# Two of the four sums of weights of a pair of column tiles are written into the plain weights' PSUM buffers

## The chip, the core and the metric

One core of a Trainium2 chip runs the kernel. The metric is the device time of one execution in microseconds (us); the kernel's time is the median of three executions. The engines are PE (matmuls; PEld are its weight loads), DVE, ACT and POOL, which work on tiles of 128 partitions, and SP, which issues the DMAs. SBUF is the working memory. PSUM is the memory that PE writes its sums to; in this kernel DVE and ACT also read and write it, POOL does not.

## What is computed

Causal attention (2 x 12 heads, 448 rows, 64 columns each), a gated layer with RMS norm (768 to 1536 and back) and a layer with a squared ReLU (768 to 2048 and back), all in float32:

```python
scores = scale * np.matmul(q, k.transpose(0, 1, 3, 2))
...
attn = attn / (np.sum(attn, axis=-1, keepdims=True) + 1e-09)
return np.matmul(attn, v).astype(np.float32)
...
xn = x / rms * rms_g
g = xn @ w_gate
silu = g * (1.0 / (1.0 + np.exp(-g)))
val = xn @ w_val
return (silu * val @ w_out).astype(np.float32)
...
h = np.maximum(x @ w_in, 0.0)
return (h * h @ w_out).astype(np.float32)
```

## The kernel before

**Numbers in two parts.** A float32 operand is split into a rounded high part and the rest (the low part), and each product of a weight tile with an activation tile is three matmuls of 128x128 by 128x448: high-high, high-low, low-high. `form` (called 7 times per pair of weight tiles, below) makes the parts of a weight: a cast for the high part (line 241 on ACT, 239 on POOL) and a subtraction for the low part (line 637, on DVE or POOL), both into one of 8 buffers `ring`. `parts` does the same for an activation tile (high: lines 241 and 239; low: line 526, on DVE or POOL), into `part`.

**Seven products for eight.** `halves` takes two column tiles of a weight matrix (a and b, each 768 rows by 128 columns of it, laid out as 128 partitions x 768, and split into halves a11, a12 and a21, a22) and multiplies them with the activations in a scheme with seven block products instead of eight. It needs four sums of weights:

```python
s1 = minus(a21, a22, da + 3, plus=True)
s2 = minus(s1, a11, da + 4)
...
s3 = minus(a11, a21, da + 6)
...
s4 = minus(a12, s2, da + 9)
```

The seven products of a pair stand on PE in the order p1 (a11), p2 (a12), p6 (s2), p5 (s1), p7 (s3), p4 (a22), p3 (s4), nine matmuls each. There are 29 such pairs: 10 for the gate and value matrices, 5 for the first output matrix, 8 for the second layer's input matrix `w2i`, 6 for its output matrix; one pair (the first) uses other buffers. The other column tiles are multiplied plainly (`whole_tiles`, `whole`).

**Where the weights lie.** The weights come as raw 8-byte pairs by DMA into `raw` (2 buffers). `weights` turns them back into float32: two ACT activations (line 600 into the plain buffer, line 605 inside `raw`) and a DVE step (line 610). The plain buffer is one of two called `s`: 1024 columns in PSUM each, of which 768 are used; a takes one, b the other. The half a21 alone goes into an `st` buffer instead (5 buffers in SBUF, 384 columns each), so that a sum of two weights always has one operand in PSUM and one in SBUF: its half of b's PSUM buffer holds an intermediate that is dead once a21 is made. The four sums (`minus`, line 664, always on DVE when an operand is in `s`) go into `st` as well. So a pair takes five `st` buffers. A `form` whose source is in `st` may run its high part on ACT or POOL and its low part on DVE or POOL. From a source in `s` the high part runs on ACT and the low part on DVE alone.

**What else is on DVE and POOL.** Differences of activations (`differences`, line 681), additions of a finished PSUM sum (banks `m`) to what came before (lines 723, 767, 938, 991), the gate's steps (lines 773 to 795), the squared ReLU (line 1001). Lines 723 and 938 also free a bank, and PE waits for them when it goes on in that bank.

**What sets the order.** `Order` is a planner that runs when the program is built: each step has a due time, the engines it may run on with an assumed cost each, what it waits for and which buffers it takes; the planner goes through assumed time and writes each engine's instructions in a fixed order. It also keeps a term for the port of SBUF that DVE and POOL share (`port=True`, set for a step whose operands are all in SBUF). An engine then runs its instructions strictly in that order, so an edit to one step can move everything behind it. All transfers are issued from SP's queue.

Of the kernel before, what the change touches and what calls it, by code (L numbers as in the profile page):

```python
# [17 lines left out]
B, H, S, D = 2, 12, 448, 64  # L18
DM, DF1, DF2 = 768, 1536, 2048
P = 128  # L20
# [25 lines left out]
class Order:  # L46
# [8 lines left out]
    def buf(self, pool):  # L55
        return Buf(pool)
# [5 lines left out]
    def add(self, due, opts, f, after=(), new=(), uses=(), mode=None, begin=0.0, prev=(), port=False):  # L62

        t = dict(due=due, opts=opts, f=f, port=port, after=[a for a in after if a], new=list(new), uses=list(uses) + list(new),
                 mode=mode, begin=begin, end=None, eng=None, i=len(self.tasks), prev=[a for a in prev if a])
        for b in t["uses"]:
            b.left += 1
        self.tasks.append(t)  # L70
        return t

    def chain(self, due, opts, f, after=(), new=(), prev=(), **kw):

        t = self.add(due, opts, f, after, new, prev=[self.last.get(b.pool) for b in new] + list(prev), **kw)
        for b in new:
            self.last[b.pool] = t
        return t
# [90 lines left out]
def tile_attention_moe_moe2(ctx: ExitStack, tc: tile.TileContext, qk, v, wg, wv, wo, w2i, w2o, rms_g, out):  # L169
# [29 lines left out]
    add, chain, buf = order.add, order.chain, order.buf  # L199
# [34 lines left out]
    def E(c):  # L234
        return {"A": nc.scalar, "D": nc.vector, "P": nc.gpsimd}[c]
# [18 lines left out]
    for i, fill in enumerate((1.0, -1.0e9 * float(D) ** 0.5)):  # L254
        for k in range(2):
            for sl in (slice(0, D), slice(D, P)):
                t = half[sl, 2 * i + k]
# [8 lines left out]
    for i in range(NV):  # L266
        t = atc.tile([P, 4, 2 * D], F32, name=f"vt{i}")
# [3 lines left out]
    for i in range(2):  # L271
        t = atc.tile([P, 2, 512], F32, name=f"p2t{i}")
# [14 lines left out]
    def D_(n):  # L287
        return 0.15 + n / 960

    def P_(n, two=False):  # L290
        return 0.2 + 0.0021 * n if two else 0.22 + 0.0009 * n
# [363 lines left out]
        return add(due, {"E": 0.61 * n}, f, [tw] + [x[1] for x in xs[:n]] + list(after), new=[bank] if first else [],  # L655
                   uses=[bw] + [x[0] for x in xs[:n]] + ([] if first else [bank]), mode="f")

    def minus(a, b, due, plus=False):

        bs = buf("st")  # L660

        def f(e):
            x, y = (t[0].tile[:, t[1]:t[1] + 3 * P] for t in (a, b))
            (E(e).tensor_add if plus else E(e).tensor_sub)(bs.tile, x, y)  # L664

        sb = "s" not in (a[0].pool, b[0].pool)
        t = chain(due, {**({"P": P_(3 * P, True)} if sb else {}), "D": D_(3 * P)}, f, [a[2], b[2]], new=[bs],
                  uses=[a[0], b[0]], port=sb)
        return bs, 0, t

    def differences(x, due, prev=(), both=False):

# [25 lines left out]
    def halves(a, b, f, due, done, scale=1.0, begin=0.0, home="s", sums=None, end=False):  # L698
# [4 lines left out]
        da = due - 18  # L703
        ca, t = weights(a, NCC, da, begin, home)
        a11, a12 = (ca, 0, t), (ca, 3 * P, t)
        a21, a22 = weights(b, NCC, da + 1, begin, home, True)
        fa11, fa12 = form(a11, 3, da + 2), form(a12, 3, da + 2)
        s1 = minus(a21, a22, da + 3, plus=True)
        s2 = minus(s1, a11, da + 4)
        fs2, fs1 = form(s2, 3, da + 5), form(s1, 3, da + 5)  # L710
        s3 = minus(a11, a21, da + 6)
        fs3 = form(s3, 3, da + 7)
        fa22 = form(a22, 3, da + 8)
        s4 = minus(a12, s2, da + 9)
        fs4 = form(s4, 3, da + 10)
        x, z, y = buf("m"), buf("m"), buf("m")

# [25 lines left out]
        if end:  # L743
            sums[0][1] = k4 = snap(x, p7, due + 9 - SOON, 1, 0)
            x = buf("m")
# [123 lines left out]
    for k in range(2 * NE):  # L869
        due = 40 + 8.0 * k  # L870
        c, t = weights((wg, wv)[k % 2][k // 2], NCC, due, due, "wt")
# [8 lines left out]
    f = differences(xf, 1012.0)  # L880
    f.update(B11=xs[0][:3], B21=xs[0][3:], B22=xs[1][3:])
    due = 1020.0
# [96 lines left out]
    due = seven(wo, 0, g, yf, due)  # L979
    hx = halved(hf, NCC, highs(g))  # L980
    due = seven(wo, NCC, hx, yf, due, n=NCC // 2 - 1)
    hy = [[parts(hf[1][NCC + i], due - 5 + i, highs(hx)) for i in range(3)]]
    due = whole(wo, NCC, NCC, [hx["B11"] + hx["B21"], hy[0] + hx["B22"]], yf, due, NCC - 2)
    f = halved(yf, 0, highs(hy))
# [32 lines left out]
    due = whole(w2o, 0, 4, hx, of, due)  # L1017
    f = halved(h2, 4, highs(hx), True)
    due = seven(w2o, 4, f, of, due)
    g = halved(h2, 10, highs(f))  # L1020
    due = seven(w2o, 10, g, of, due, True)
# [43 lines left out]
```

## Time and profile before

| | |
|---|---|
| median of 3 executions | 562.68 us (559.97, 562.68, 563.57) |
| the profiled execution | 564.28 us, of which the span from first to last instruction is 562.5 us |
| PE / PEld busy | 545.7 us (97%) / 475.4 us (85%) |
| DVE busy | 495.5 us (88%) |
| ACT / POOL busy | 379.6 us (67%) / 280.8 us (50%) |
| granted TensorE clock, whole span | 0.997 of full speed (2.4 GHz) |

A matmul is pipelined: it is shown as 367 ns long on average, while the next starts about 0.2 us after it. PE's busy share therefore hides short stops. The number of matmuls that start in a stretch of time is the better measure of PE's pace. The attention takes the first 117 us; the matmuls of line 652 (all the big products) follow until 558.6 us.

### The profile page before, as it was taken

The numbers are of one execution on the slowest core, as the hardware profiler recorded it, in microseconds if no ns is written. First come the engines' busy times: TensorE is split into PE (matmuls) and PEld (weight loads), VectorE is DVE, ScalarE is ACT, GpSimd is POOL, SyncE is SP. The second block draws the span as 40 slices with busy tenths as digits, with TensorE's granted clock in tenths as the row PEclk, the third lists the DMA queues.
The fourth block names the chain that finished last, engine by engine and source line by source line (L and its number), as shares of the span: only waits on it lengthen the run. The fifth ranks groups of instructions, "written<-read, shape, count | busy, mean of one in ns | idle before, by whom it ended". The sixth has DMA issues, their size and how long they took to land.

```text
span 562.5 us, 8893 instructions
## 1 busy us (share of the span) xinstructions
PE 545.7 (97%) x3056; PEld 475.4 (85%) x3056; DVE 495.5 (88%) x862; ACT 379.6 (67%) x802; POOL 280.8 (50%) x322
## 2 busy tenths in 40 slices
PE   7999999999899999999999999899999999999997
PEld 4666666899899999999989789789999999999896
DVE  4778988699998998999999999999888887999983
ACT  4678888566766666668787576666766876758510
POOL 4466776343630442147488488331212871687710
PEclk9899999999999999999999999999999999999999
DMA  6255323303233333344253143025432344431422
GB/s 180 83 174 188 113 67 128 114 2 113 89 136 114 113 112 118 123 141 132 106 162 119 57 158 123 2 112 174 148 128 76 112 144 128 160 103 66 145 84 82
DMA packets 19501, 65.06 MB, mean 116 GB/s; under 512 B 2048, under 2 KB 8960, under 8 KB 19456
## 3 DMA queue, kind: packets, MB, share of 16 engines
q1 hardware_dynamic: 19376, 64.27, 34.4%
q8 instruction: 24, 0.39, 0.3%
q10 hardware_dynamic: 80, 0.23, 0.2%
q14 instruction: 21, 0.17, 0.1%
HBM read 61.74 MB, written 2.75 MB: 115 GB/s over the span
## 4 chain that ended last, share of the span: by engine, by line
PE 68%; DVE 23%; issue 3%; POOL 3%; ACT 2%; DMA 1%; POOLq 0%; ACTq 0%; DVEq 0%
PE m L652 53%; DVE ring L637 6%; DVE part L526 5%; PE t L439 3%; PE o L477 3%; PE s L336 3%; PE s L852 2%; PE s L349 2%; DVE st L664 2%; DVE row L681 2%; DVE row L938 2%; DVE s L610 2%; POOL p L423 1%; ACT ring L241 1%; DVE row L723 1%
## 5 line engine op out<-in xcount | busy, mean ns | idle before, releaser
L652 PE MATMUL m<-part,ring 128*128 128x448 f32 x2115 | 436.0, 367 | 5.6 <-DVE part L526 2.4
L652 PEld LDWEIGHTS m<-part,ring 128*128 128x128 f32 x2115 | 395.9, 188 | 45.6 <-DVE part L526 4.6
L526 POOL TENSOR_TENSOR part<-row,part 128x448 fp32r<-128x448 f32 x78 | 99.3, 1292 | 45.9 <-ACT part L241 44.9
L681 POOL TENSOR_TENSOR row<-row 128x448 f32<-128x448 f32 x52 | 65.6, 1276 | 25.4 <-DVE row L792 19.7
L241 ACT CAST ring<-st 128x384 fp32r<-128x384 f32 x93 | 46.4, 512 | 35.7 <-DVE st L664 25.4
L605 ACT ACTIVATE raw<-raw 128x768 uint32<-128x768 uint8 (+1 forms) x70 | 62.6, 894 | 11.1 <-DMA raw<-in_wv 4.4
L637 DVE TENSOR_TENSOR ring<-st,ring 128x384 fp32r<-128x384 f32 x96 | 68.1, 736 | 1.5 <-ACT ring L241 1.1
L241 ACT CAST part<-row 128x448 fp32r<-128x448 f32 x111 | 58.9, 570 | 14.0 <-DVE row L681 11.4
L239 POOL TENSOR_SCALAR ring<-st 128x384 fp32r<-128x384 f32 x23 | 12.4, 537 | 108.7 <-DVE st L664 62.7
L600 ACT ACTIVATE s<-raw 128x768 f32<-128x768 f32 (+1 forms) x64 | 54.1, 849 | 10.2 <-DVE ring L637 8.8
L241 ACT CAST ring<-s 128x384 fp32r<-128x384 f32 x100 | 43.9, 469 | 18.3 <-DVE s L610 9.6
L526 DVE TENSOR_TENSOR part<-row,part 128x448 fp32r<-128x448 f32 x62 | 54.7, 902 | 0.7 <-POOL part L239 0.4
L610 DVE SCALAR_TENSOR_TENSOR s<-s,raw 128x768 uint32<-128x768 uint32 (+1 forms) x64 | 48.6, 760 | 3.7 <-ACT s L600 2.4
L637 DVE TENSOR_TENSOR ring<-s,ring 128x384 fp32r<-128x384 f32 x100 | 51.2, 531 | 0.5 <-ACT ring L241 0.3
L282 ACT COPY snap<-m 128x448 f32<-128x448 f32 x47 | 25.0, 532 | 29.7 <-PE m L652 29.0
L372 DVE TENSOR_REDUCE mx<-s 128x2 f32<-128x256 f32 (+2 forms) x36 | 23.8, 687 | 14.0 <-PE s L352 9.0
L423 POOL TENSOR_SCALAR p<-p,r 128x128 f32<-128x128 f32 (+1 forms) x48 | 24.3, 524 | 20.8 <-DVE r L413 18.0
L664 DVE TENSOR_TENSOR st<-st,s 128x384 f32<-128x384 f32 x56 | 30.7, 548 | 1.1
L664 DVE TENSOR_TENSOR st<-s,st 128x384 f32<-128x384 f32 x56 | 30.0, 548 | 0.3 <-ACT ring L241 0.2
L637 POOL TENSOR_TENSOR ring<-st,ring 128x384 fp32r<-128x384 f32 x20 | 21.7, 1087 | 15.4 <-ACT ring L241 14.5
L336 PE MATMUL s<-qk 64*128 64x128 f32 (+2 forms) x144 | 27.0, 456 | 1.6 <-DMA qk<-in_qk 0.9
L938 DVE TENSOR_TENSOR row<-m,row 128x448 f32<-128x448 f32 x36 | 22.3, 621 | 5.2 <-PE m L652 4.7
(98 smaller groups left out, 586.6 us busy)
## 6 DMA issues: line engine op xcount, KB each, us to landing
raw<-in_w2i SPq DMA_DIRECT2D x16, 768.0 KB, 4.2
raw<-in_wg SPq DMA_DIRECT2D x12, 768.0 KB, 4.3
raw<-in_wv SPq DMA_DIRECT2D x12, 768.0 KB, 4.3
raw<-in_wo SPq DMA_DIRECT2D x12, 768.0 KB, 4.3
raw<-in_w2o SPq DMA_DIRECT2D x12, 768.0 KB, 4.4
qk<-in_qk SPq DMA_DIRECT2D x11, 448.0 KB, 3.4
raw<-in_w2o SPq DMA_DIRECT2D x6, 512.0 KB, 3.7
out_t<-row SPq DMA_DIRECT2D x12, 224.0 KB, 1.9
```

Of the source, the lines that this page charges most:

```text
L241: eng.copy(o, i)
L336: nc.tensor.matmul(s[:, h, o:o + n], z["qk"][BOTH[h], 0, qs], z["qk"][BOTH[h], 1, :n], start=True, stop=False)
L423: E(e).tensor_scalar(t, t, z["r"][:, k:k + 1], 1.0, ALU.mult, ALU.mult)
L526: E(e).tensor_sub(bs.tile[:, 1], bf.tile, bs.tile[:, 0].bitcast(F32))
L600: nc.scalar.activation(bt.tile[:, :n * P], br.tile[:, :n * P, 1].bitcast(F32), AF.Prelu, scale=2.0 ** -112, alpha=2.0 ** 32)
L605: nc.scalar.activation(br.tile[:, :n * P, 0], b, AF.Copy, scale=1.0 / 32, bias=-31.0 / 64)
L610: nc.vector.scalar_tensor_tensor(dst.tile.bitcast(U32) if dst else u, u, 3, br.tile[:, a:b, 0], ALU.logical_shift_left, ALU.bitwise_or)
L637: E(e).tensor_sub(br.tile[:, 1, :n], num(), br.tile[:, 0, :n].bitcast(F32))
L652: nc.tensor.matmul(bank.tile[:, :S], bw.tile[:, a, i], x[:, c], start=first and i == 0 and k == 0, stop=last and i == n - 1 and k == 2, sk ...
L664: (E(e).tensor_add if plus else E(e).tensor_sub)(bs.tile, x, y)
L681: E(e).tensor_sub(bs.tile, a[0].tile, b[0].tile)
L938: nc.vector.tensor_add(bf.tile, bank.tile[:, :S], snap.tile if snap else bf.tile)
```

## The change

`minus` gets an argument `to`: a place that exists already. With it the sum is written there and takes no `st` buffer. s3 = a11 - a21 goes into the dead half of b's PSUM buffer, after a21 is made; s4 = a12 - s2 goes over a12 in a's PSUM buffer, after a12's low part is made. s1 and s2 stay in `st`. The steps that form s3 and s4 now read PSUM, so each has ACT for its high part and DVE for its low part, and a's buffer is in use until the parts of s4 are made.

```diff
-    def minus(a, b, due, plus=False):
+    def minus(a, b, due, plus=False, to=None):
 
-        bs = buf("st")
+        bs, o = (to[0], to[1]) if to else (buf("st"), 0)
 
         def f(e):
             x, y = (t[0].tile[:, t[1]:t[1] + 3 * P] for t in (a, b))
-            (E(e).tensor_add if plus else E(e).tensor_sub)(bs.tile, x, y)
+            (E(e).tensor_add if plus else E(e).tensor_sub)(bs.tile[:, o:o + 3 * P], x, y)
 
         sb = "s" not in (a[0].pool, b[0].pool)
-        t = chain(due, {**({"P": P_(3 * P, True)} if sb else {}), "D": D_(3 * P)}, f, [a[2], b[2]], new=[bs],
-                  uses=[a[0], b[0]], port=sb)
-        return bs, 0, t
+        opts = {**({"P": P_(3 * P, True)} if sb else {}), "D": D_(3 * P)}
+        if to:
+            t = add(due, opts, f, [a[2], b[2], to[2]], uses=[a[0], b[0]] + ([bs] if bs not in (a[0], b[0]) else []), port=sb)
+        else:
+            t = chain(due, opts, f, [a[2], b[2]], new=[bs], uses=[a[0], b[0]], port=sb)
+        return bs, o, t
...
-        s3 = minus(a11, a21, da + 6)
+        s3 = minus(a11, a21, da + 6, to=(a22[0], 0, a21[2]))
         fs3 = form(s3, 3, da + 7)
         fa22 = form(a22, 3, da + 8)
-        s4 = minus(a12, s2, da + 9)
+        s4 = minus(a12, s2, da + 9, to=(ca, 3 * P, fa12[2]))
```

Lines from 674 on carry higher numbers in the changed kernel: 681 is 684 there, 723 is 727, 938 is 942, 991 is 995, 1001 is 1005. PE's products keep their order. On DVE and POOL the planner moves a good deal.

**First place: DVE around 316 to 325 us**, where the first output matrix changes over from pairs to plain column tiles. Lines 723 and 938 (727 and 942) add a finished sum and free its bank; line 526 is the low part of an activation; line 610 a weight. Before:

```order
L610 SCALAR_TENSOR_TENSOR s<-s,raw 128x768
L526 TENSOR_TENSOR part<-row,part 128x448
L723 TENSOR_TENSOR row<-m,row 128x448
L637 TENSOR_TENSOR ring<-s,ring 128x384
L526 TENSOR_TENSOR part<-row,part 128x448 x3
L723 TENSOR_TENSOR row<-m,row 128x448
L938 TENSOR_TENSOR row<-m,row 128x448
L637 TENSOR_TENSOR ring<-s,ring 128x384
L938 TENSOR_TENSOR row<-m,row 128x448
```

The same stretch in the changed kernel:

```order
L610 SCALAR_TENSOR_TENSOR s<-s,raw 128x768
L727 TENSOR_TENSOR row<-m,row 128x448
L942 TENSOR_TENSOR row<-m,row 128x448
L637 TENSOR_TENSOR ring<-s,ring 128x384
L727 TENSOR_TENSOR row<-m,row 128x448
L637 TENSOR_TENSOR ring<-s,ring 128x384
L526 TENSOR_TENSOR part<-row,part 128x448
L637 TENSOR_TENSOR ring<-s,ring 128x384
L610 SCALAR_TENSOR_TENSOR s<-s,raw 128x768
L942 TENSOR_TENSOR row<-m,row 128x448
```

Before, four low parts of activations stand among these rows, three of them in a row ahead of an addition; now one stands there, and the others have moved to POOL or to other places on DVE.

**Second place: DVE between two pairs of `w2i`** (about 390 to 400 us). Lines 991 and 1001 (995 and 1005) finish a column of the pair that PE is at; line 610 makes the next pair's weights, and the last row its first two low parts. Before:

```order
L610 SCALAR_TENSOR_TENSOR s<-s,raw 128x768
L991 TENSOR_TENSOR row<-m,snap 128x448
L1001 SCALAR_TENSOR_TENSOR row<-row 128x448
L991 TENSOR_TENSOR row<-m,snap 128x448
L1001 SCALAR_TENSOR_TENSOR row<-row 128x448
L610 SCALAR_TENSOR_TENSOR st<-s,raw 128x384
L610 SCALAR_TENSOR_TENSOR s<-s,raw 128x384
L637 TENSOR_TENSOR ring<-s,ring 128x384 x2
```

In the changed kernel:

```order
L995 TENSOR_TENSOR row<-m,snap 128x448
L1005 SCALAR_TENSOR_TENSOR row<-row 128x448
L637 TENSOR_TENSOR ring<-s,ring 128x384
L995 TENSOR_TENSOR row<-m,snap 128x448
L1005 SCALAR_TENSOR_TENSOR row<-row 128x448
L610 SCALAR_TENSOR_TENSOR s<-s,raw 128x768
L610 SCALAR_TENSOR_TENSOR st<-s,raw 128x384
L610 SCALAR_TENSOR_TENSOR s<-s,raw 128x384
L637 TENSOR_TENSOR ring<-s,ring 128x384 x2
```

The step that makes a's weights has moved behind both finished columns, and the low part of s4 of the running pair stands ahead of it, since a's buffer is held until then.

## Rows read from the trace of the kernel before

**Rows 1.** The page, busy time of the engines over the span (us, share, instructions).

```profile
PE 545.7 (97%) x3056; PEld 475.4 (85%) x3056; DVE 495.5 (88%) x862; ACT 379.6 (67%) x802; POOL 280.8 (50%) x322
```

**Rows 2.** Busy time by stretch: us, each engine's time (instructions), clock, DMA.

```profile
150.00:280.00 130.00, 130.00 (x643) 120.45 (x643) 122.18 (x211) 92.38 (x169) 52.27 (x53) 1.00 0.38 128
283.00:367.00 84.00, 80.03 (x379) 69.95 (x379) 82.51 (x123) 59.07 (x110) 57.41 (x50) 1.00 0.30 102
370.00:530.00 160.00, 160.00 (x776) 145.30 (x775) 142.25 (x245) 114.47 (x211) 80.81 (x80) 1.00 0.37 127
```

**Rows 3.** Timeline of PE, unbroken runs: start, length, matmuls [idle before, releaser].

```profile
147.73 163.08 PE L652 MATMUL m<-part,ring 128*128 128x448 f32 x799 [1.42 <-ACT snap L282]
311.21 4.39 PE L652 MATMUL m<-part,ring 128*128 128x448 f32 x20 [0.40 <-DVE part L526]
315.96 2.07 PE L652 MATMUL m<-part,ring 128*128 128x448 f32 x9 [0.36 <-DVE row L938]
318.55 5.79 PE L652 MATMUL m<-part,ring 128*128 128x448 f32 x27 [0.53 <-DVE row L723]
324.57 27.38 PE L652 MATMUL m<-part,ring 128*128 128x448 f32 x133 [0.22 <-DVE row L938]
353.12 4.53 PE L652 MATMUL m<-part,ring 128*128 128x448 f32 x21 [1.17 <-DVE part L526]
...
366.41 166.20 PE L652 MATMUL m<-part,ring 128*128 128x448 f32 x803 [0.41 <-DVE part L526]
532.85 25.78 PE L652 MATMUL m<-part,ring 128*128 128x448 f32 x126 [0.24 <-DVE row L723]
```

**Rows 4.** Timeline of DVE, 309 to 325 us: start, length of the group.

```profile
311.08 0.54 DVE L637 TENSOR_TENSOR ring<-st,ring 128x384 fp32r<-128x384 f32 x1
...
316.59 1.28 DVE L526 TENSOR_TENSOR part<-row,part 128x448 fp32r<-128x448 f32 x1
317.80 0.61 DVE L723 TENSOR_TENSOR row<-m,row 128x448 f32<-128x448 f32 x1
...
318.80 3.53 DVE L526 TENSOR_TENSOR part<-row,part 128x448 fp32r<-128x448 f32 x3
```

**Rows 5.** DVE by shape, whole span: count, busy us, mean ns, idle before.

```profile
L637 DVE TENSOR_TENSOR ring<-st,ring 128x384 fp32r<-128x384 f32 x96 | 68.1, 736 | 1.5 <-ACT ring L241 1.1 <-POOL ring L239 0.4
L526 DVE TENSOR_TENSOR part<-row,part 128x448 fp32r<-128x448 f32 x62 | 54.7, 902 | 0.7 <-POOL part L239 0.4 <-ACT part L241 0.2
L637 DVE TENSOR_TENSOR ring<-s,ring 128x384 fp32r<-128x384 f32 x94 | 49.9, 547 | 0.5 <-ACT ring L241 0.3
...
L610 DVE SCALAR_TENSOR_TENSOR s<-s,raw 128x384 uint32<-128x384 uint32 x28 | 15.7, 562 | 0.6
L1001 DVE SCALAR_TENSOR_TENSOR row<-row 128x448 f32<-128x448 f32 x22 | 15.5, 703 | 0.8
...
L610 DVE SCALAR_TENSOR_TENSOR st<-s,raw 128x384 uint32<-128x384 uint32 x28 | 15.3, 547 | 1.7 <-ACT raw L605 1.7
```

**Rows 6.** DVE by shape, 283 to 367 us only.

```profile
L637 DVE TENSOR_TENSOR ring<-st,ring 128x384 fp32r<-128x384 f32 x18 | 18.0, 1018 | 0.4 <-POOL ring L239 0.4
L526 DVE TENSOR_TENSOR part<-row,part 128x448 fp32r<-128x448 f32 x16 | 16.4, 1046 | 0.0
L637 DVE TENSOR_TENSOR ring<-s,ring 128x384 fp32r<-128x384 f32 x17 | 9.0, 546 | 0.1
...
L610 DVE SCALAR_TENSOR_TENSOR s<-s,raw 128x768 uint32<-128x768 uint32 x7 | 6.7, 958 | 0.0
L681 DVE TENSOR_TENSOR row<-row 128x448 f32<-128x448 f32 x7 | 5.9, 848 | 0.0
L664 DVE TENSOR_TENSOR st<-s,st 128x384 f32<-128x384 f32 x10 | 5.3, 546 | 0.0
```

**Rows 7.** POOL by shape, whole span, the low parts of activations.

```profile
L526 POOL TENSOR_TENSOR part<-row,part 128x448 fp32r<-128x448 f32 x78 | 99.3, 1292 | 45.9 <-ACT part L241 44.9
```

**Rows 8.** Waits by engine and line: us in total, times, longest.

```profile
ACT s L600 <- DVE ring L637: 8.8, 9, 3.4
```

## The prediction

> **What bounds the kernel now.** I began with the busy shares [rows 1]. PE is at 97%, so a change on DVE can give back only what PE stops for, plus whatever changes PE's pace. The question is where PE stops, and for whom.
>
> The table by stretch [rows 2] answers the first half, if matmuls are counted. At a granted clock of 1.00 (the 2.4 GHz level) 643 matmuls fit into the 130 us from 150 to 280, one per 0.2022 us. From 370 to 530 there are 776 in 160 us, one per 0.2062 us (each count is one or two too high at its edges). Between them, 283 to 367, there are 379 in 84 us: at 0.2022 us they need 76.6 us, so 7.4 us are lost. The timeline of PE's unbroken runs [rows 3] shows them as a series of stops from 311 to 366 us, each released by DVE (line 526, 723 or 938), one per row and two rows left out. Outside it there are two stops, at 147.73 (1.42 us idle) and at 532.85 (0.24 us).
>
> The second half: in that stretch DVE is busy 82.51 of 84 us [rows 2], against 122.18 of 130 before it. DVE's queue is the bound there. Why it is so slow there is seen by comparing shapes. Forming a low part from `s` (PSUM) takes 547 ns over the whole span and 546 in the stretch. The same size from `st` (SBUF) takes 736 over the span and 1018 in the stretch [rows 5, 6]. Low parts of activations, also all in SBUF, go from 902 to 1046. So an instruction with both inputs in SBUF loses up to half a microsecond there, and one that reads PSUM loses nothing. One form from `st` that met no POOL work took 0.54 us [rows 4]. POOL does its own SBUF work at that time, 57.41 us of 84 [rows 2]; that the two disturb each other is my reading of these rows.
>
> A third thing matters for the size of any answer: PE has two paces, 0.2022 and 0.2062 us, at the same clock. The slow one holds from the stop at 366.41 to the one at 532.85: 803 matmuls in 166.44 us [rows 3]. 4 ns on 803 matmuls are 3.2 us. I see the pace change only at stops, and nothing in the rows tells which one PE will take.
>
> **The change, part by part.**
>
> *The sums themselves.* 56 sums (28 pairs, s3 and s4; the first pair's buffers lie in SBUF) write PSUM now. Nothing is added or removed. The trace has no subtraction of two weights that writes `s`; its bounds are line 610 into `s`, 562 ns, and into `st`, 547 [rows 5], same size and inputs. So 0 to 15 ns each, 0.8 us over the span at most. I take 0: the ten sums of the bound stretch would cost 0.15 us, and elsewhere DVE's slack of 8 us in 130 [rows 2] hides it. Without that cover it is 0.8 us.
>
> *The forms of s3 and s4.* Their low parts now read PSUM and are DVE's alone. By the instruction orders, DVE's low parts from `st` fall from 96 to 48 and those from `s` rise from 94 to 150. The planner gives POOL other work for what it loses: the low parts of activations on DVE fall from 62 to 47, and POOL's rise from 78 to 93. At 1292 ns [rows 7] the fifteen are 19.4 us more for POOL, which is busy 50% of the span [rows 1].
>
> *What that is worth.* Only the bound stretch counts. Between the addition at 283.3 us and the line 991 at 370.3 us the orders give, for DVE:
> - low parts from `st` 18 to 10: 8 x 1.00 us (18.0 us for 18, [rows 6]) = -8.0
> - low parts from `s` 19 to 30: 11 x 0.53 (9.0 for 17) = +5.8
> - low parts of activations 16 to 11: 5 x 1.03 (16.4 for 16) = -5.1
> - differences, line 681, 7 to 9: 2 x 0.84 (5.9 for 7) = +1.7
> - sums, line 664, 18 to 20: 2 x 0.53 (5.3 for 10) = +1.1
> - one more square (0.70, line 1001, [rows 5]) and two fewer copies (0.61 each, as line 723 of the same size, [rows 4]) = -0.5
>
> That is -5.0 us on a queue that is full. The bounds: if POOL's extra work makes the remaining SBUF instructions dearer in the same measure, nothing is left; if every collision goes with the eight low parts, PE gets back all of its stops. These are below the 7.4 us, since the slow pace has a share of it: 4 ns on 379 matmuls at most, 1.5 us. So the range is 0 to about 6.8.
>
> *Where it arrives.* At 315.96, 318.55 and 324.57 PE waits for additions (lines 938, 723, 938), which free banks [rows 3]. Just ahead of such additions DVE does a low part of 1.28 us at 316.59, and three in 3.53 us at 318.80 [rows 4]. In the new order one stands there instead of four (first place). Those three stops, idle 0.36 + 0.53 + 0.22, are longer by about 0.2 us each, since PE's idle time begins only when the last matmul has drained: about 1.7 us, and I expect nearly all of it back. The one at 311.21 waits for a low part (about 0.6); the new order puts that row ahead of the two low parts from `st` that preceded it, so this one too should go. The later stops: the 133 matmuls from 324.57 to 353.12 need 26.9 of 28.55 us, and the next 54 (21 in their row, 33 in the two rows left out) 10.9 of 13.29 us, so about 4.0 us are lost. There s1 and s2 are still formed from `st`, so I expect half, 2.0 us. Together 1.7 + 0.6 + 2.0 = **4.3 us**, which agrees with the -5.0 from the other side, and I take it.
>
> *What is moved the wrong way.* a's `s` buffer is now held until s4 is formed. ACT already waits for DVE's low parts before it can fill that buffer, 8.8 us in 9 waits [rows 8]. In the new order (second place) the next pair's weights are made after both finished columns. From the end of p5, which releases the second of these additions, PE has p7, p4 and p3 left: 27 matmuls, 5.5 us. DVE needs in that time 0.61 (line 991, as line 723), 0.70 (line 1001), 0.96 + 0.56 + 0.55 (line 610) and 0.53 (the first low part) [rows 4 to 6]: 3.9 us. 1.6 us remain, so this costs nothing as long as nothing else comes between. Before, a's weights were made ahead of the first column, and there was far more room.
>
> *The first stop*, 147.73, stays: the orders there differ by one more low part from `s` ahead of the difference it hangs on (+0.5) and a POOL low part fewer. I take 0. SP's queue moves one load of the last pair behind the first store; the product that needs it comes more than 100 matmuls (20 us) after. Nothing.
>
> *A rule against it.* The Trainium skill, "Perfetto Trace Analysis", section "Optimizing Scalar/DVE Operations", gives DVE an overhead of about 60 ns for SBUF and 125 for PSUM. By it the 10 sums and 11 low parts that go to PSUM in the stretch would cost 65 ns more each, 1.4 us, and 5.0 would be 3.6, an estimate. The rows here show no such step: 546 ns from PSUM [rows 6], and 0.54 us for an undisturbed form from SBUF at 311.08 [rows 4]. The trace disagrees, and I leave the sum.
>
> **The sum.** The profiled execution took 564.28 us (span 562.5). 564.28 - 4.3 = 560.0. It lies 1.6 us above the median of the three, which a difference in pace can explain. Off the median, 562.68 - 4.3 = 558.4, and that is the basis I use: **558.5 us**.
>
> **The rivals.**
> - *No gain.* POOL's 15 more low parts collide with what DVE still does in SBUF, or the pace falls at an early stop: 643 matmuls from 150 to 280 at 4 ns more are 2.6 us. For it: s1 and s2 stay in `st`, and POOL's waits leave it room to come at any time. Against it: eight of 18 exposed forms are gone. Time: 562.0.
> - *Gain and fast pace.* If PE leaves the stops of 353 to 366 at the fast pace, 3.2 us more come off: about 555. For it: the stretch up to 280 ran so. Against: nothing decides it here.
> - *Slower.* The next pair's weights come too late at the second place. It decides when DVE or ACT puts more than the spare 1.6 us into that path, as one collided low part (1.0) and a line 610 (0.96) would. Every pair of the gate, `w2i` and the second half of w2o repeats it: 0.4 us on some 21 pairs are 8 us, 570. Against it: the rows in that path read PSUM and do not lengthen.
> - *PSUM dearer.* If each of the 21 instructions that go to PSUM in the stretch cost a tenth more than the 546 ns of rows 6, the gain is 1.1 us smaller: 559.6. Against it: 562 ns against 547 [rows 5]. The Trainium skill's rule above points this way.
>
> **How the numbers follow.** Forecast 0.55 (its own range 555.5 to 561.5), no gain 0.22, fast pace 0.12, slower 0.08, PSUM dearer 0.03. About 1% (5.6 us) is what a measurement of this kernel can tell from no change: below 557.05 is faster, above 568.3 slower. Faster: the fast pace and three tenths of the forecast, 0.28. Slower: 0.08. The same: 0.64. For 8 in 10 the range takes in the no-gain case with its scatter and the fast pace, and leaves the slower one out: 554.0 to 564.5.
>
> **What would show it.** Right: between 283 and 370 us the low parts from `st` number about 10, PE's stops at 311 to 325 are gone, and the count of matmuls in 84 us rises from 379 towards 400. Wrong: line 526 or 681 on DVE above 1.1 us each there; a repeated stop at every p1 of a pair with ACT's line 600 or DVE's line 610 as releaser; or an equal number of stops with a pace of 0.206 where it was 0.202.

## The result

The changed kernel takes **555.83 us** (median of 7 executions, 553.28 to 559.01) against 562.27 for the kernel before on the same chip (7 executions, 559.97 to 563.71): ratio **0.9899, 95% interval 0.9864 to 0.9934**. It is faster by about 1%, 2.7 us below the forecast and inside the range. Two more measurements of it, in experiments below, gave 0.9939 and 0.9961; why they differ is part of the story. By the three measurements the kernel is faster by 0.4 to 1.0%. Three executions with a mean granted clock of 0.56 to 0.75 and one of the kernel before that took 568.33 us are in no ratio.

The profiled execution of the changed kernel took 555.83 us, of which the span is 553.9. The table by stretch, in the form of [rows 2]:

```profile
150.00:280.00 130.00, 130.00 (x643) 120.36 (x642) 121.24 (x214) 90.59 (x168) 51.37 (x52) 1.00 0.38 126
283.00:367.00 84.00, 82.66 (x408) 76.16 (x407) 81.17 (x130) 61.80 (x116) 64.80 (x58) 1.00 0.34 115
370.00:530.00 160.00, 159.79 (x789) 147.76 (x788) 143.69 (x247) 110.22 (x208) 79.83 (x78) 1.00 0.37 123
```

In the bound stretch 408 matmuls start where 379 did. From 370 to 530 there are 789 for 776, and PE hardly stopped there in either kernel: that is pace. The timeline of PE's unbroken runs, in the form of [rows 3]:

```profile
117.37 29.34 PE L652 MATMUL m<-part,ring 128*128 128x448 f32 x144
148.62 149.87 PE L652 MATMUL m<-part,ring 128*128 128x448 f32 x738 [1.90 <-DVE uu L793]
299.83 177.24 PE L652 MATMUL m<-part,ring 128*128 128x448 f32 x873 [1.34 <-ACT snap L282]
477.27 73.23 PE L652 MATMUL m<-part,ring 128*128 128x448 f32 x360 [0.21 <-DVE row L727]
```

All the stops from 311 to 366 us are gone. Three are left: the first (1.90 for 1.42), a new one at 299.83, and a small one at 477. DVE in the bound stretch, by shape, as in [rows 6]:

```profile
L637 DVE TENSOR_TENSOR ring<-s,ring 128x384 fp32r<-128x384 f32 x30 | 16.3, 548 | 1.6 <-ACT ring L241 1.5
L637 DVE TENSOR_TENSOR ring<-st,ring 128x384 fp32r<-128x384 f32 x10 | 11.1, 1135 | 0.0
L684 DVE TENSOR_TENSOR row<-row 128x448 f32<-128x448 f32 x9 | 8.5, 943 | 0.0
L526 DVE TENSOR_TENSOR part<-row,part 128x448 fp32r<-128x448 f32 x11 | 8.4, 765 | 0.0
...
L664 DVE TENSOR_TENSOR s<-s,st 128x384 f32<-128x384 f32 x10 | 5.6, 557 | 0.0
L664 DVE TENSOR_TENSOR st<-st,s 128x384 f32<-128x384 f32 x10 | 5.5, 549 | 0.1
```

The counts are those of the order (30, 10, 9, 11). A low part made from PSUM takes 548 ns as before. What reads two SBUF operands takes 765 to 1135, and these means moved: the low parts from `st` went from 1018 to 1135, the differences from 848 to 943, the low parts of activations from 1046 to 765. A sum costs 557 ns into `s` and 549 into `st`. ACT's waits for DVE's low parts, which answer to [rows 8]:

```profile
ACT ring L241 <- DVE ring L637: 11.8, 8, 3.0
ACT s L600 <- DVE ring L637: 6.1, 11, 1.0
```

Line 600 waits less than before. Line 241, a cast, waits 11.8 us; in the kernel before it was

```profile
ACT ring L241 <- DVE ring L637: 4.0, 4, 1.9
```

**How the runs are compared.** For each profile I took the starts of the 2115 matmuls of line 652 and split the time from the first to the last into a base (2114 spacings of 202.7 ns and the length of the last matmul, the same 428.9 us in all kernels), what starts more than 230 ns apart lose ("stops", the lower clock included), and what the rest lose against 202.7 ns ("pace"). The two paces can be told by their rhythm: 206, 207, 207 ns evenly, or a cycle of five near 199, 207, 202, 203, 202. In us:

| kernel | ratio to before [95%] | first to last | stops | pace |
|---|---|---|---|---|
| before | | 441.7 | 9.0 | 3.8 |
| before_again | | 441.5 | 9.0 | 3.6 |
| after | 0.9899 [0.9864, 0.9934] | 433.1 | 4.3 | -0.1 |
| after_again | 0.9939 [0.9916, 0.9962] | 436.0 | 7.2 | -0.1 |
| after_third | 0.9961 [0.9932, 0.9989] | 438.3 | 8.4 | 1.0 |
| no_pool | 1.0025 [0.9993, 1.0056] | 443.4 | 10.3 | 4.2 |
| s3_sbuf | 0.9982 [0.9948, 1.0016] | 439.5 | 4.8 | 5.8 |
| s4_only | 0.9979 [0.9953, 1.0006] | 441.2 | 8.5 | 3.7 |
| banks_before | 0.9997 [0.9968, 1.0026] | 444.4 | 8.1 | 7.4 |
| banks_again | 0.9935 [0.9910, 0.9959] | 436.0 | 7.2 | 0.0 |
| late_after | 0.9872 [0.9837, 0.9908] | 435.8 | 4.4 | 2.5 |
| late_banks | 0.9894 [0.9856, 0.9931] | 437.5 | 3.4 | 5.3 |
| late_s3a | 0.9844 [0.9805, 0.9882] | 433.1 | 3.0 | 1.2 |

The ratio is over several executions, the other columns are of the one profiled. Of the 8.6 us between the first and the third row, 4.7 are stops and 3.9 pace. By place, the 4.7 are 6.4 us less at the stops of 311 to 366 us and 0.4 less at small ones near 282, against 0.5 more at the first stop and 1.6 at the new one.

### The profile page after: what moved, and what is told of

Read it like the earlier page. It is cut to its first block, busy times and chain, and to the rows that moved or that the text cites. A ratio compares the mean times of both kernels' runs of the same rounds, so it can differ in the third digit from the quotient of the medians.

```text
span 553.9 us, 8846 instructions
## 1 busy us (share of the span) xinstructions
PE 539.3 (97%) x3056; PEld 476.6 (86%) x3056; DVE 485.9 (88%) x858; ACT 375.1 (68%) x799; POOL 286.0 (52%) x326
## 4 chain that ended last, share of the span: by engine, by line
PE 77%; DVE 15%; ACT 2%; DMA 2%; POOL 2%; issue 2%; POOLq 0%; DVEq 0%; ACTq 0%; SPq 0%
PE m L652 65%; DVE ring L637 4%; PE t L439 3%; PE o L477 3%; PE s L336 3%; DVE part L526 3%; PE s L349 2%; POOL p L423 1%; DVE row L684 1%; DMA raw<-in_wv 1%; DVE row L577 1%; DMA qk<-in_qk 1%; DVE s L610 1%; DVE st L664 1%; DVE mx L370 1%
## 5 line engine op out<-in xcount | busy, mean ns | idle before, releaser
L652 PE MATMUL m<-part,ring 128*128 128x448 f32 x2115 | 429.7, 365 | 3.5 <-DVE uu L793 1.9
L526 POOL TENSOR_TENSOR part<-row,part 128x448 fp32r<-128x448 f32 x93 | 114.6, 1252 | 34.6 <-ACT part L241 31.7
L241 ACT CAST ring<-s 128x384 fp32r<-128x384 f32 (+1 forms) x156 | 69.5, 473 | 35.6 <-DVE s L610 11.9
L637 DVE TENSOR_TENSOR ring<-s,ring 128x384 fp32r<-128x384 f32 (+1 forms) x156 | 80.4, 539 | 6.2 <-ACT ring L241 5.5
L239 POOL TENSOR_SCALAR ring<-st 128x384 fp32r<-128x384 f32 x17 | 8.7, 513 | 114.2 <-DVE st L664 92.6
L526 DVE TENSOR_TENSOR part<-row,part 128x448 fp32r<-128x448 f32 x47 | 37.5, 818 | 0.6 <-POOL part L239 0.4
L637 DVE TENSOR_TENSOR ring<-st,ring 128x384 fp32r<-128x384 f32 x48 | 37.8, 818 | 0.0
L239 POOL TENSOR_SCALAR part<-row 128x448 fp32r<-128x448 f32 x37 | 25.8, 700 | 20.9 <-PE m L652 17.1
L241 ACT CAST ring<-st 128x384 fp32r<-128x384 f32 x41 | 20.1, 511 | 20.6 <-DVE st L664 16.3
L664 DVE TENSOR_TENSOR s<-s,st 128x384 f32<-128x384 f32 x56 | 31.4, 560 | 0.5
```

The lines of the kernel that those rows point to most:

```text
L239: eng.tensor_scalar(o, i, 1.0, 1.0, ALU.mult, ALU.mult)
L241: eng.copy(o, i)
L526: E(e).tensor_sub(bs.tile[:, 1], bf.tile, bs.tile[:, 0].bitcast(F32))
L637: E(e).tensor_sub(br.tile[:, 1, :n], num(), br.tile[:, 0, :n].bitcast(F32))
L652: nc.tensor.matmul(bank.tile[:, :S], bw.tile[:, a, i], x[:, c], start=first and i == 0 and k == 0, stop=last and i == n - 1 and k == 2, sk ...
L664: (E(e).tensor_add if plus else E(e).tensor_sub)(bs.tile[:, o:o + 3 * P], x, y)
```

## The experiments

### Each kernel again

*before_again* is the kernel before, unchanged, run once more.

> The kernel before, once more, for a second profile of it. If PE's pace (one matmul per 0.2022 or 0.2062 us) belongs to the kernel, the stretch 370 to 530 us holds 776 matmuls again and 150 to 280 us holds 643. If it belongs to the single execution, one of the two counts differs: 789 in the first or 631 in the second. The stops between 311 and 366 us should be there in either case, about 6 us in all.

It took 561.96 us. The timeline of PE's unbroken runs shows the same stops, and the same long slow run at the end:

```profile
309.01 4.33 PE L652 MATMUL m<-part,ring 128*128 128x448 f32 x20 [0.86 <-DVE part L526]
...
322.37 27.88 PE L652 MATMUL m<-part,ring 128*128 128x448 f32 x133 [0.22 <-DVE row L938]
350.85 4.53 PE L652 MATMUL m<-part,ring 128*128 128x448 f32 x21 [0.60 <-DVE part L526]
...
364.14 166.17 PE L652 MATMUL m<-part,ring 128*128 128x448 f32 x803 [0.50 <-DVE part L526]
```

803 matmuls in 166.17 us answer to 803 in 166.20 [rows 3], and the stretches of [rows 2] hold 643 and 776 matmuls again. So in these two executions the pace of the long runs repeated. It is not fixed throughout: the 133 matmuls after 322.37 took 27.88 us here and 27.38 before.

*after_again* and *after_third* are the changed kernel, unchanged, on the chips of the other experiments.

> The changed kernel, once more. If its gain is in the stops alone, 556 us again (ratio 0.99) with three stops, at about 148, 300 and 477 us, whatever the pace. If the fast pace of its first profile was luck, this profile shows 776 instead of 789 matmuls from 370 to 530 us or 631 instead of 643 from 150 to 280 us, and its span is 2 to 6 us longer.

> The changed kernel once more, beside the two layouts. Two of its executions ran wholly at the fast pace of 202.7 ns a matmul. If the pace belongs to the kernel's order, it does so again, with stops at matmuls 144, 882 and 1755 alone, and the time is 0.990 to 0.994 of before. If the pace is drawn anew at each stop, some hundred matmuls may run at 206.7 ns here: up to 4 us longer, 0.997.

They are 0.9939 and 0.9961. The pace is the fast one again (a loss of -0.1 and 1.0 us), the stops at 300 and 477 us are there again; what differs is the first stop. In after_third, PE's run behind the stop:

```profile
148.23 153.74 PE L652 MATMUL m<-part,ring 128*128 128x448 f32 x738 [3.18 <-DVE uu L793]
```

The timeline of DVE ahead of it:

```profile
141.80 2.93 DVE L637 TENSOR_TENSOR ring<-st,ring 128x384 fp32r<-128x384 f32 x2
```

And PE's table by stretch behind the stop:

```profile
148.00:153.00 5.00, 4.77 (x13) 4.27 (x14) 4.21 (x8) 3.18 (x6) 2.00 (x2) 0.50 0.12 28
153.00:158.00 5.00, 5.00 (x24) 4.51 (x23) 2.36 (x5) 1.83 (x4) 1.34 (x2) 0.88 0.80 288
```

The same table for the first profile of the changed kernel, where the stop was 1.90 us:

```profile
148.00:153.00 5.00, 4.38 (x22) 4.10 (x23) 4.59 (x8) 3.97 (x8) 1.61 (x2) 1.00 0.17 22
153.00:158.00 5.00, 5.00 (x26) 4.64 (x25) 4.37 (x9) 2.77 (x6) 1.77 (x2) 1.00 0.75 292
```

After a stop of 3.18 us the granted clock is 0.50 (the 1.2 GHz level) from 148 to 153 and 13 matmuls start, not 22. After the 1.90 us it stayed at 1.00. Counted by the starts of the matmuls, 2.1 us are lost there in the first profile and 5.0 and 6.1 in after_again and after_third (1.7 in the kernel before).

It is DVE that is late. It reaches line 793 30.5 us after the first matmul of line 652 in the first profile and 31.8 us in after_third. The same two low parts from `st` took, in the first profile,

```profile
142.54 1.97 DVE L637 TENSOR_TENSOR ring<-st,ring 128x384 fp32r<-128x384 f32 x2
```

That is 1.0 us less than in after_third, but the low part of an activation behind them took 0.6 us more (1.57 for 0.97). The other 1.0 us lies 13 us earlier: one low part of an activation takes 1.58 us on DVE in after_third and 0.62 in the first profile. In both, a low part on POOL starts 0.15 us ahead of it; POOL's took 1.25 us in after_third and 2.26 in the first profile. So the same two instructions met, and it was now the one, now the other engine that lost the time.

The executions without a profile show only their mean granted clock. Of the 29 executions of this kernel (the three profiled ones among them) 12 have 0.993 or 0.994, with a mean span of 558.2 us; the other 17 have 0.996 or more and 555.2. That mean is a rough sign, since it also holds a fall of the clock in the attention that some executions have: the first profile's 0.996 comes from 13 to 18 us, where the clock is 0.66. In after_again the two low executions are no longer than the other eight (555.9 against 556.3). So the profiles show what the longer stop costs, 2.8 and 4.0 us; how much of the spread of the three ratios it makes is not shown.

### Is it POOL alone?

*no_pool*: the sums stay in SBUF, but the forms of s3 and s4 may not go to POOL, as in the change.

```diff
-    def form(src, n, due):
+    def form(src, n, due, pool=True):
...
-        sb = b.pool != "s"
+        sb = b.pool != "s" and pool
...
-        fs3 = form(s3, 3, da + 7)
+        fs3 = form(s3, 3, da + 7, False)
...
-        fs4 = form(s4, 3, da + 10)
+        fs4 = form(s4, 3, da + 10, False)
```

> The kernel before, all four sums in SBUF, but the planner may not put the forms of s3 and s4 on POOL. Planner theory (POOL is freed for the low parts of activations): most of the gain, 557 to 558. Port theory: nothing or a loss, since DVE gets more work with both inputs in SBUF: 562 to 566.

1.0025: no gain, the time that the port theory expected. Its table by stretch:

```profile
150.00:280.00 130.00, 127.67 (x617) 115.24 (x616) 122.24 (x206) 87.48 (x157) 53.32 (x54) 1.00 0.36 122
283.00:367.00 84.00, 82.99 (x401) 74.22 (x400) 81.94 (x130) 57.27 (x107) 64.14 (x58) 1.00 0.35 117
```

The bound stretch is nearly as good as in the changed kernel (401 for 408), but 26 matmuls are missing from 150 to 280, and there are 10.3 us of stops in all. The planner's new order only moved the stops.

### The order of after, with s3 in SBUF

*s3_sbuf* keeps the instruction order of the changed kernel. s3 is written to an SBUF tile of its own (`sh`) and formed from there; s4 stays in PSUM. (Two tiles of four columns in the norm also share one buffer now.) The part of the edit that writes s3:

```diff
+            if to and bs.pool == "s" and o == 0:
+                sh[bs, o] = pw.tile([P, 3 * P], F32, tag=f"sh{o}", name="sh", bufs=1)
+                E(e).tensor_sub(sh[bs, o], x, y)
+                return
...
```

> The changed kernel with its instruction order, only that s3 is written to an SBUF tile of its own and formed from there; s4 stays in PSUM. Port theory (the forms that read PSUM no longer collide with POOL): about 5 of the 15 low parts moved in the bound stretch are exposed again at 1.0 instead of 0.55 us, so 2 to 3 us on DVE come back there: about 558.5. Planner theory (what counts is the order that the planner made): no change, 556. It also takes away the wait of a22's high part for s3's low part, which by itself would give up to 1.6 us (554).

DVE by shape in 283 to 367 us (line 641 is 637 of the changed kernel):

```profile
L641 DVE TENSOR_TENSOR ring<-s,ring 128x384 fp32r<-128x384 f32 x24 | 13.0, 547 | 0.8 <-ACT ring L241 0.8
...
L526 DVE TENSOR_TENSOR part<-row,part 128x448 fp32r<-128x448 f32 x11 | 9.5, 859 | 0.0
...
L641 DVE TENSOR_TENSOR ring<-sh,ring 128x384 fp32r<-128x384 f32 x6 | 5.7, 953 | 0.0
```

One run of PE:

```profile
314.53 173.69 PE L656 MATMUL m<-part,ring 128*128 128x448 f32 x837 [1.51 <-DVE row L735]
```

This is the price of the place, at the same order: a low part of s3 takes 953 ns from SBUF where others take 547 from PSUM, 2.4 us on six, and the eleven of line 526 take 859 where they took 765, 1.1 more. It comes back as one stop of 1.51 us at 314.53, for a DVE addition. But the stop at 300 us is not there, so all stops together are 4.8 us, hardly more than in the changed kernel. Of the 6.5 us that the kernel before lost from 311 to 366 us, 2.0 are lost here: the order keeps the rest away, also with s3 in SBUF. Whether it would with both sums in SBUF was not run. The time, 560.42 us (0.9982), is above all that were expected; in the profiled execution the reason is 5.8 us of slow pace.

### One of the two sums

*s4_only*: s4 goes into PSUM, s3 stays in SBUF, and the planner makes its own order. Against the kernel before, with `minus` as in the change:

```diff
-        s4 = minus(a12, s2, da + 9)
+        s4 = minus(a12, s2, da + 9, to=(ca, 3 * P, fa12[2]))
```

> Half of the change: s4 alone goes to PSUM, s3 stays in SBUF, and the planner makes its own order (DVE low parts from st 96 to 76, from s 100 to 128, activation low parts on DVE 62 to 60). Theory that the gain is DVE time in 283 to 367 us: half of the forms are gone, but only 2 activation low parts leave DVE in place of 15, so DVE gets back under half: stops of 311 to 366 us go from about 6.5 to about 3 us, 0.993 to 0.997. Rival, that the order which the planner makes keeps the stops away, wherever the sums lie: this order is closer to that of before, so about as many stops as before and 0.997 to 1.003.

0.9979, no measured gain. The bound stretch by itself is better, as its row shows; the stops of 311 to 366 us lose 3.0 us for 6.5, as the first theory expected:

```profile
283.00:367.00 84.00, 82.42 (x398) 73.94 (x397) 82.39 (x131) 57.06 (x105) 63.59 (x58) 1.00 0.34 113
```

But it has a first stop with 2.69 us of idle, with the lower clock behind it, and the slow pace for some 900 matmuls (3.7 us in all). There is no stop at 300 us. So the time came out as the rival had it, for reasons that neither theory named.

### What makes the new stop at 300 us

The timeline of DVE ahead of it, in the changed kernel:

```profile
295.58 2.73 DVE L637 TENSOR_TENSOR ring<-st,ring 128x384 fp32r<-128x384 f32 x2
298.23 0.54 DVE L637 TENSOR_TENSOR ring<-s,ring 128x384 fp32r<-128x384 f32 x1
```

ACT at that time:

```profile
298.86 0.48 ACT L241 CAST ring<-s 128x384 fp32r<-128x384 f32 x1 [2.11 <-DVE ring L637]
299.24 0.54 ACT L282 COPY snap<-m 128x448 f32<-128x448 f32 x1
```

ACT's cast of a22 waits 2.11 us until DVE has done the low part of s3 (298.23), which stands behind two low parts from `st` that take 2.73 us beside POOL. Behind the cast in ACT's queue is the copy of a bank that PE waits for. s3 lies beside a22 in b's buffer, at columns 0 to 383 and 384 to 767: the first bank (512 columns) holds all of one and a part of the other. My first theory was the shared bank. *banks_after* and *banks_again* put the second half at column 512:

```diff
-        a11, a12 = (ca, 0, t), (ca, 3 * P, t)
+        H2 = 512 if home == "s" else 3 * P
+        a11, a12 = (ca, 0, t), (ca, H2, t)
...
```

> The changed kernel with one difference: the two halves of a pair's plain weights start in two PSUM banks (columns 0 and 512 of the buffer), not at columns 0 and 384 where the second half begins in the first bank. The order of the instructions is the same. Theory: the 1.6 us stop of PE at 300 us comes from a wait that the change made, ACT's cast of a22 (line 241 of the changed kernel) for DVE's low part of s3, which lies in the same bank. Then the stop goes, ACT's waits for DVE low parts (11.8 us in 8 of line 241) fall to under half, and the span is about 1.6 us shorter than that of the changed kernel beside it: near 0.987 to 0.991 of before. Rival: the stop comes from DVE's late low parts alone (2.73 us for two that ran beside POOL); then a stop of over 1 us stays at matmul 882 and the time is that of the changed kernel. A third case: the stop goes, but PE takes the slow pace (206.7 ns in place of 202.7) for some hundred matmuls after another stop; then up to 4 us come back.

> The changed kernel with the two halves in two banks, once more, for a profile at full clock. Same-bank theory: no stop at matmul 882 (1.5 us in all three profiles of the changed kernel), ACT's waits of line 241 for DVE low parts under half of 12 us; time 0.990 to 0.994 of before, with the first stop of 2 to 3.4 us still there. Rival: DVE's own lateness makes the stop: it stays above 1 us.

*banks_after* gave 0.9937 [0.9905, 0.9970]. ACT and PE are read from banks_again, the same kernel, where the granted clock at this place is 1.00. ACT there:

```profile
299.53 0.48 ACT L241 CAST ring<-s 128x384 fp32r<-128x384 f32 x1 [2.10 <-DVE ring L649]
299.90 0.54 ACT L282 COPY snap<-m 128x448 f32<-128x448 f32 x1
```

And PE:

```profile
300.50 177.23 PE L664 MATMUL m<-part,ring 128*128 128x448 f32 x873 [1.36 <-ACT snap L282]
```

Wait and stop are the same to 0.02 us, as the rival had it. The theory of the shared bank falls; that DVE's late low parts hold PE by themselves is still possible. As a control, *banks_before* has that layout in the kernel before:

> The kernel before with the same layout of two banks. The theory has no same-bank wait of ACT for DVE low parts of sums here, since the sums lie in SBUF; ACT's line 241 waits only 4.0 us in 4 for them. So no change: 0.997 to 1.003 of before, stops between 311 and 366 us as before. Rival: the layout in two banks brings something by itself (line 600 and line 610 writing two banks): 0.99 to 0.995.

0.9997: nothing, as expected. (Its profile has 7.4 us of slow pace, the kernel before 3.8: at the same order too the pace can differ by 3.6 us.)

The second theory is that this kernel, as built, lets ACT's and DVE's accesses to one PSUM *buffer* wait for each other, whatever the bank. It is tested together with the first stop.

### The first stop, and the buffer

*late_after* keeps the order of the changed kernel, but writes three low parts of one pair (s3, a22, s4) on DVE behind the line 793 that PE waits for at the first stop. The three are needed by products three and more places further on.

```diff
-        done(0, 0, z, k1[0], [p2, k1[1]], due + 4 - SOON, False)
+        r0 = done(0, 0, z, k1[0], [p2, k1[1]], due + 4 - SOON, False)
+        if late:
+            for fm in (fs3, fa22, fs4):
+                fm[2]["hold"] = r0
...
```

A step with `hold` is written behind the step it names.

> The changed kernel with one difference: on DVE, at the first stop of PE (148 us), the three low parts of s3, a22 and s4 of the second pair are written behind the line 793 that frees the bank, not ahead of it; every other instruction stands where it stood. Theory: in the changed kernel the first stop is 2.1 us in one profile and 3.4 in two, because DVE is late by low parts that met POOL; after the long one the granted clock falls to the lower level for 10 to 25 matmuls at some 170 ns more each, 1.5 to 4 us, so the kernel has two kinds of executions (clock 0.994 and 0.999). With about 1.5 us of low parts out of the way the stop is 0.5 to 2.0 us, the clock does not fall, most executions show a clock of 0.996 or more, and the time is 2 to 4 us below the changed kernel: 0.988 to 0.992 of before. Rival: PE waits there for ACT's copy or POOL, not for DVE's queue: the stop stays above 2 us and the time at 0.994 to 0.996. Second rival: the stop moves to product 19 or later, where the moved low parts are needed: a new stop at matmul 162 to 216.

**0.9872**, 555.81 us. The timeline of DVE at the first stop, in the changed kernel:

```profile
145.93 1.01 DVE L637 TENSOR_TENSOR ring<-s,ring 128x384 fp32r<-128x384 f32 x2
146.86 0.61 DVE L684 TENSOR_TENSOR row<-row 128x448 f32<-128x448 f32 x1
147.39 0.55 DVE L637 TENSOR_TENSOR ring<-s,ring 128x384 fp32r<-128x384 f32 x1
147.86 0.61 DVE L793 SCALAR_TENSOR_TENSOR uu<-m,snap 128x448 f32<-128x448 f32 x1
```

In late_after (lines 793, 637 and 652 are 806, 647 and 662 there):

```profile
145.69 0.61 DVE L806 SCALAR_TENSOR_TENSOR uu<-m,snap 128x448 f32<-128x448 f32 x1
146.22 1.47 DVE L647 TENSOR_TENSOR ring<-s,ring 128x384 fp32r<-128x384 f32 x3
```

PE's runs behind the stop, and behind the one at 300 us:

```profile
146.44 151.08 PE L662 MATMUL m<-part,ring 128*128 128x448 f32 x738 [0.82 <-ACT part L251]
298.89 177.24 PE L662 MATMUL m<-part,ring 128*128 128x448 f32 x873 [1.36 <-ACT snap L292]
```

The table by stretch:

```profile
145.00:150.00 5.00, 4.18 (x20) 3.51 (x20) 4.89 (x11) 3.19 (x6) 0.00 (x0) 1.00 0.01 3
```

The stop's idle time falls to 0.82 us. Two small ones of 0.17 and 0.34 now stand ahead of it, and by the starts of the matmuls the three lose 2.1 us together, as much as the one stop in the first profile of the changed kernel. What the move takes away is the long form of the stop: DVE comes to the line that PE waits for 30.5 us after the first matmul, and the three low parts behind it (1.47 us) would have made it 31.9, an estimate, as late as in after_third. The clock stays at 1.00.

All 18 executions of the three kernels with this move have a mean clock of 0.996 or more. Of the 50 executions of the order without it (the changed kernel's 29 and 21 of the two-bank layout), 20 have less; on the chip of late_after and late_banks it is 5 of 12 without the move (banks_again) and none of 12 with it. The long stop need not show in the mean: banks_again's profile has it, 3.17 us with the clock at 0.66 from 148 to 153, at a mean of 0.997. On that chip the ratio is 0.9872 with the move, just below the range expected, and 0.9935 for banks_again. No new stop came where the moved parts are needed. *late_banks* adds the two banks:

> The same move of three low parts, and the two halves of the plain weights in two PSUM banks. If both stops (148 and 300 us) have the causes named, it gains the sum: about 1.6 us below the run with the move alone, 0.985 to 0.989 of before, with no stop at matmul 882 and ACT's waits of line 241 for DVE low parts under half of 12 us. If the pace is the larger matter, it may lie anywhere within 0.985 to 0.997, and the profile's count of matmuls at 206.7 ns says so (4 ns each).

0.9894. Its stop at 300 us is 0.59 us in place of 1.36, but ACT's cast still waits 1.68 us for DVE, so the wait is there; its pace lost 5.3 us where late_after's lost 2.5, and a PE that comes later waits less, as I read it. So it settles nothing about the banks.

*late_s3a* is late_after with one operand changed: s3 is written over a11, in a's buffer, where s4 lies too, and b's buffer is left to a22.

```diff
-        s3 = minus(a11, a21, da + 6, to=(a22[0], 0, a21[2]))
+        s3 = minus(a11, a21, da + 6, to=(a22[0], 0, a21[2]), at_=ca)
...
```

> The changed kernel with the move of three low parts at the first stop, and s3 written over a11 in a's buffer, not over the place beside a22 in b's. The order of the instructions stays the same. The two layouts in separate banks left the stop at matmul 882 at 1.5 us, so a shared bank is not what ACT's cast of a22 waits for. New theory: it is the shared buffer. Whatever the bank, the program lets ACT's cast of a22 wait for DVE's low part of s3, since both read one PSUM buffer. With s3 in a's buffer that wait is gone from the program, the cast of a22 waits only for the product that frees its ring place, and ACT copies the bank about 0.9 us earlier: stop at 882 0.4 to 0.8 us in place of 1.53, span 0.7 to 1.1 us shorter at the same pace, 0.985 to 0.989 of before. Rival: DVE's two low parts that take 2.7 us beside POOL hold PE by themselves: the stop stays above 1.3 us. Pace: up to 4 ns on each of 2115 matmuls either way, read from the profile.

**0.9844 [0.9805, 0.9882]**, 554.76 us against 562.34: the lowest ratio of all, though its interval overlaps that of late_after. The timeline of DVE ahead of the place of the stop:

```profile
294.13 2.71 DVE L647 TENSOR_TENSOR ring<-st,ring 128x384 fp32r<-128x384 f32 x2
```

ACT's cast of a22:

```profile
295.94 0.48 ACT L251 CAST ring<-s 128x384 fp32r<-128x384 f32 x1 [0.31 <-PE m L662]
```

PE's run from the first stop on:

```profile
147.86 327.09 PE L662 MATMUL m<-part,ring 128*128 128x448 f32 x1611 [0.84 <-ACT part L251]
```

The bound stretch:

```profile
283.00:367.00 84.00, 83.91 (x415) 77.35 (x414) 82.09 (x134) 63.64 (x117) 62.54 (x56) 1.00 0.34 113
```

DVE's two low parts take 2.71 us as before, so the rival (that these hold PE) is out. ACT's cast now waits 0.31 us for PE, the stop at 300 us is gone, not only shortened, and 1611 matmuls run without idle time from 147.86 on (one start comes 0.25 us late, at 312 us). s3_sbuf, where s3 has a buffer of its own, has no stop at 300 us either. It was the buffer. In this kernel a layout in separate banks did not remove the wait (2.10 us), another buffer did. The Trainium skill, "PSUM — Partial Sum Buffer", section "PSUM bank collisions raise a hardware error", says to guard PSUM by bank and quadrant. The waits of this kernel go further than that.

## Why the prediction was right, and where it was not

- **What bounds the kernel** (stops from 311 to 366 us, made by DVE's SBUF instructions beside POOL): right. The counts came as the orders gave them, and all stops of that stretch went. That POOL's work is what makes these instructions long was my reading; the kernel before shows it directly. Of its 96 low parts from `st` on DVE, the 57 that no POOL instruction overlaps take 549 ns on average and the 39 that one overlaps take 1008; low parts from `s` take 547 and 548. The Trainium skill, "SBUF — State Buffer", section "Who interferes with whom", has the rule for it: a DVE instruction with two SBUF inputs contends with a GpSimd one that reads SBUF, and one with at most one SBUF input, outside the two-port modes, does not. The rows agree (1135 against 548 ns in the changed kernel).
- **The prices:** that of a low part from PSUM held (546 and 548 ns). Those of the SBUF instructions did not, 1135 for 1018 and 765 for 1046 ns; low parts and differences together still went from 49.3 to 44.3 us, so these errors cancelled.
- **The size, 4.3 us:** too small for that stretch. From 311 to 366 us the stops lost 6.5 us and now lose nothing; the 29 matmuls more (5.9 us at 0.2027) are net of the new stop. The failed term is the half I took at 353 to 366 us ("I expect half, 2.0 us"): these stops lost 3.7 us, and all of it came back. (The upper bound of 6.8 is not what 7.4 less 1.5 gives, 5.9; by the starts of the matmuls the stops of 283 to 367 us do lose 6.8.) I credited the place of the sums with all of the gain there. In s3_sbuf, with s3 in SBUF and s4 in PSUM, 4.4 of the 6.5 us stay away, so the order that the planner makes once the forms leave POOL has a large part in it; no_pool shows that not every such order does it. What the order gives without either sum in PSUM stays open.
- **"The first stop stays. I take 0":** failed. I counted one low part more (+0.5) and one POOL low part less, as an exchange. The stop cost 0.5 us more in the first profile and, with the lower clock, 3.3 and 4.5 more in the two others. In after_third DVE lost another 1.3 us in low parts that met POOL's: from the first matmul of line 652 to the line that PE waits for it took 30.0 us in the kernel before, 30.5 in the first profile and 31.8 in after_third. POOL also does four differences (line 684) in a row there where it did three; that this matters is not shown.
- **Waits of ACT:** I looked at ACT's line 600, which waits for a's buffer, and that one got shorter (8.8 to 6.1 us). The cost came at line 241 (4.0 to 11.8): s3 beside a22 in one buffer ties ACT's cast to DVE's queue, 1.6 us of stop. It was not among the parts.
- **The pace:** "nothing in the rows tells which one PE will take", and I gave 0.12 to the fast one. It came in all three profiles of the changed kernel, nearly throughout, and gave 3.9 of the 8.6 us of the profiled pair. What sets it is still open. I saw it change at stops; it mostly repeats with the same kernel, but kernels with the same order can differ: s3_sbuf by 5.9 us from the changed kernel, banks_before by 3.6 from the one before, late_banks by 2.8 from late_after. No run here was made to set it.
- **Second place** (next pair's weights later, no cost) and **PSUM dearer**: right. There is no repeated stop, and sums into PSUM cost 8 ns more than into SBUF in the stretch, within the 0 to 15 given.

So the forecast's mechanism is there, and the size is partly luck: more stops removed and a faster pace on one side, two new costs on the other. Against a forecast gain of 4.2 us, the three measurements gave 6.4, 3.2 and 2.0.

## What to carry to other kernels

When an operand moves into a buffer that another engine reads, look for what the build makes wait on that buffer, and put together in one buffer what the same queue needs in the same order. Where a planner makes the order, a large part of an edit's effect may be the order: hold the order fixed and change one place at a time to tell the two apart. A stop that grew by 1.3 us cost about 3 here, since the clock fell behind it.

## What was not expected of the hardware

Behind stops of 2.7 to 3.2 us (after_again, after_third, banks_again, s4_only) the granted clock of PE fell to 0.50 for some microseconds of steady work; behind stops of 1.3 to 1.9 us it stayed at 1.00. At a granted clock of 1.00, matmuls of the same shape run at 202.7 or 206.7 ns each, for hundreds in a row. When a low part on DVE and one on POOL meet, it is not always the same engine that loses: the same pair took 1.58 and 1.25 us in one execution, 0.62 and 2.26 in another.
